# Value products of banded attention issued once per group of heads and query tile, with their sums in the exponentials' banks

## The chip, the cores and the metric

The kernel runs on one core of a Trainium2 chip. The metric is the time of one execution on the device, in microseconds, as the median of several runs. TensorE (PE) multiplies matrices into PSUM, where this kernel rotates eight banks, each of 128 partitions by 512 float32 numbers; its weight loads are shown as PEld. VectorE (DVE), ScalarE (ACT) and GpSimd (POOL) do the rest of the arithmetic. SyncE (SP) issues the DMAs, in order, in one queue.

## The reference

Two branches work on the same 2048 rows and are mixed by a gate. Branch A is attention with 32 heads of 16 numbers, in which a query sees itself and the 255 keys before it; branch B is a dense layer, gelu, and a second dense layer. The kernel is given everything in float32.

```python
g = sigmoid((x * gate_w).sum(-1, keepdims=True))          # x: 2048 x 512
q, k, v = split(x @ wqkv)                                 # 32 heads of 16
scores = q @ k.T / 4, kept where 0 <= query - key < 256, else -1e9
a = (softmax(scores) @ v) @ wo                            # wo: 512 x 512
b = gelu(x @ w1 + b1) @ w2 + b2                         # 512 -> 1792 -> 512
out = g * a + (1 - g) * b
```

## The kernel before

Dense products are made of three matmuls each (`mm3`, lines 95 to 97), on numbers split into a high and a low part, over query tiles of T = 512 rows (four tiles, `c` or `t`). The dense work is one long generator: queries, keys and values of all tiles (qk, v), then eight turns of the two dense layers, half of the 1792 columns at a time. A turn has seven first-layer products (u), each followed by a chain of gelu steps on ACT, DVE and POOL, then four second-layer products (y). At the end stand the attention's output products (a).

Attention goes over eight groups of four heads. For each group there are 16 blocks of 128 keys (`kb`), so 128 steps `u`; in each step PE does, for each of four heads `i`:

- `att_max` (m): a score matmul with queries as output rows into a bank "sm" (three of these). DVE takes the row maxima (M), eight blocks ahead of their use.
- `att_exp` (s): a score matmul with keys as output rows into a bank "st". ACT writes exp(scores) into "pt" buffers of SBUF, each for two heads, and POOL sets the corners outside the band to zero (`affine_select`, lines 427 and 430).
- `att_pvs` (p), at the third head: products of finished exponentials with values ("pv", line 455), in four column strips of 32, one for each head, accumulated over the key blocks of a query tile in one bank. At the last block of a tile ACT copies the bank to "nd" (line 466), which goes to DRAM as ND.
- `fill` (f): dense work, 2296 ns in each step, between the attention's matmuls.

A key block has 384 queries, so it feeds the query tile of its own and, for the last two blocks of a tile, also the next one. The kernel before issues pv at every second block: four pairs of block and tile at a tile's second block (two of them of the tile before it; two pairs in tile 0), two at its fourth.

After odd groups `att_norm` fetches sums (den) and numerators (num) from ND, takes the reciprocal on DVE (line 496), writes it to DRAM (RD), fetches it spread over rows (rb), multiplies (line 501) and writes OT. At the end `load_o` fetches OT, ACT and DVE split it (ot, lines 533 and 536), and `final` multiplies with wo.

The order on PE, ACT, DVE and POOL is the order in which the program is written out (`manual_schedule`). It is kept by a planned clock: `after(ns, ...)` puts a step off, `tick(ns)` moves the clock by the planned length of a matmul and runs what is due; `NORM` is the delay between the steps of `att_norm`. The DMAs on SP are ordered by the scheduler. Buffers are rotations by tag (`bufs`): whoever takes the next buffer waits until the one in it is no longer read.

Of the kernel before, what the change touches and what calls it, by code (L numbers as in the profile page):

```python
# [32 lines left out]
def gated_mix(ctx: ExitStack, tc: tile.TileContext, x, wqkv, wo, w1, b1, w2, b2, gate_w, out):  # L33
# [28 lines left out]

    identr = cp.tile([128, 128], F32R, name="identr")
    one = sb.tile([128, 128], F32, tag="x1", bufs=2, name="one")
    make_identity(nc, one)
    nc.vector.tensor_copy(identr, one)
    ident = f32(identr)
# [17 lines left out]
    nms = [cp.tile([128, RB, 32], F32R, name=f"nm{i}") for i in range(2)]  # L85
    for nm in nms:
        nc.gpsimd.memset(f32(nm), 0.0)
    vbuf = cp.tile([128, 2, NB * 68 + 16], F32, name="vbuf")
# [37 lines left out]
    def load_raw(key, early=False):  # L126
        kind, i = key
        src = {"qk": lambda: wk4[:, :, i * 128:(i + 1) * 128],
               "v": lambda: wqkv[i * 128:(i + 1) * 128, 2 * D:3 * D],
               "w1": lambda: w1k[:, :, i * 128:(i + 1) * 128],  # L130
               "w2": lambda: w2[i * 128:(i + 1) * 128],
               "wo": lambda: wo[i * 128:(i + 1) * 128]}[kind]()
        if early and kind == "v" and i < 2:
            raw = sb.tile([128, T], F32, tag="sq", bufs=2, name=f"raw_{kind}{i}")
        elif early and kind == "v":
            raw = f32(sb.tile([128, 2, T], F32R, tag="h", bufs=8, name=f"raw_{kind}{i}"))[:, 0]
        elif early:
            raw = sb.tile([128, 2, 384], F32, tag="pt", bufs=11, name=f"raw_{kind}{i}")
# [88 lines left out]
    def gate_z(t, b):  # L227
        xr = xrs.pop((t, b))
        junk = sb.tile([128, D], BF16, tag="x1", bufs=2, name=f"xj{t}_{b}")
        nb = t * NB + b  # L230
# [49 lines left out]
    def qkv(t):  # L280
# [17 lines left out]
        for n, (kind, j) in enumerate(pieces):  # L298
# [9 lines left out]
            if t == 0 and n == 10:  # L308
                nc.sync.dma_start(b2b, b2.partition_broadcast(128))
                nc.sync.dma_start(b1c, b1.rearrange("(f p) -> p f", p=128))  # L310
# [83 lines left out]
    def att_rows(g_, rb):  # L394

        need(*[("max", g_, rb * RB + b, i) for b in range(RB) for i in range(4)])
        m = Ms.pop((g_, rb))
        nm = nms[rb % 2][:, :, 0:8].rearrange("p b (i k) -> p k b i", k=2)
# [3 lines left out]
        tt = sb.tile([128, RB, 32], F32, tag="tt", bufs=2, name=f"tt{g_}_{rb}")  # L402
        nc.vector.transpose(tt.rearrange("p b c -> p (b c)"), f32(nms[rb % 2]).rearrange("p b c -> p (b c)"))

# [9 lines left out]
    def att_exp(g_, kb, i):  # L414
# [8 lines left out]
        nc.tensor.matmul(p[:, :w], ks[:, pr, s, kb * 128:(kb + 1) * 128],  # L423
# [17 lines left out]
    def att_pv(g_, kb, c):  # L441
# [6 lines left out]
        if first:  # L448
            n = g_ * NT + c - 1
            if n >= 0:  # L450
                need(("nd", *divmod(n, NT)))
            pvs[g_, c] = ps.tile([128, T], F32, tag="pv", bufs=1, name=f"pv{g_}_{c}")
        pv = pvs[g_, c]
        for i in range(4):
# [4 lines left out]
                             skip_group_check=True, tile_position=(0, 32 * i))  # L459
        tick((e - q) * 1.67 + 150)  # L460
        if kb % NB == NB - 1 and c == kb // NB:
            nd = sb.tile([128, T], F32, tag="tmp", bufs=4, name=f"nd{g_}_{c}")
            pv = pvs.pop((g_, c))
# [21 lines left out]
    def att_norm(t, c):  # L485

        v = ND[t][c].rearrange("g (i r) c -> (g i) r c", r=32)
        den = sb.tile([128, 32], F32, tag="den", bufs=2, name=f"den{t}_{c}")
        rec = sb.tile([128, 32], F32, tag="rec", bufs=2, name=f"rec{t}_{c}")
        nc.sync.dma_start(den, v[:, 16, :].rearrange("i (j c) -> i j c", c=32))  # L490
        num = sb.tile([128, T], F32, tag="tmp", bufs=4, name=f"num{t}_{c}")
        rb = sb.tile([128, T], F32, tag="tmp", bufs=4, name=f"rb{t}_{c}")
        nc.sync.dma_start(num, v[:, 0:16, :])

        def rcp():
            nc.vector.reciprocal(rec, den)
            nc.sync.dma_start(RD[t][c].rearrange("h (j c) -> (h j) c", c=32), rec)
            nc.sync.dma_start(rb, RD[t][c].unsqueeze(1).broadcast_to([8, 16, T]))
# [16 lines left out]
    def load_o(t):  # L515
# [7 lines left out]
        for c in range(NC):  # L523
            need(("o", t, c))
            if t == 0:
                raw = sb.tile([128, T], F32, tag=("x1", "sq")[c % 2], bufs=2, name=f"or{t}_{c}")
            else:
                raw = sb.tile([128, 2, 384], F32, tag="pt", bufs=11, name=f"or{t}_{c}")
                raw = raw.rearrange("p a b -> p (a b)")[:, 0:T]
# [39 lines left out]
    def mlp(n):  # L569
# [22 lines left out]
        for b in range(NB):  # L592
# [3 lines left out]
            p = ps.tile([128, D], F32, tag="d", bufs=2, name=f"y{t}_{half}{b}")  # L596
            if half == 1:
                ya = sb.tile([128, D], F32, tag="ya", bufs=2, name=f"ya{t}_{b}")
                need(("y", 0, t, b))
                nc.sync.dma_start(ya, YA[t][ts])  # L600
            for i in range(HF):
# [4 lines left out]
                if last and b == NB - 1 and later:  # L606
                    load(later.pop(0))
            def ev(p=p, b=b, ts=ts, ya=b2b if half == 0 else ya):
                y = sb.tile([128, D], F32, tag="y", bufs=1, name=f"yo{t}_{half}{b}")
                nc.vector.scalar_tensor_tensor(y, p, 0.5, ya, op0=ALU.mult, op1=ALU.add)  # L610
# [20 lines left out]
    def final(t):  # L631
# [8 lines left out]
        for b in range(NB):  # L640
            ts = slice(b * 128, (b + 1) * 128)
            nb = t * NB + b
            after(YLAND if nb == 0 else 0, scale_y, nb)
            a = sb.tile([128, 2, 384], F32, tag="pt", bufs=11, name=f"ao{nb}")
            a = a.rearrange("p a b -> p (a b)")[:, 0:D]
# [51 lines left out]
    for u in range(-LEAD, NU):  # L697
# [35 lines left out]
START = 117e3  # L733
NORM = 6000
GELU = (700, 1500, 2300, 3300, 4200, 5000)
# [29 lines left out]
```

## Time and profile before

| | us |
|---|---|
| median of three runs | 807.09 (806.85 to 811.15) |
| the profiled execution | 806.06 |
| its span, first to last instruction | 804.4 |
| PE busy in the span | 783.4 |
| DVE busy | 526.3 |
| ACT busy | 427.0 |
| POOL busy | 357.9 |

A line of a group reads: source line, engine, operation, output from inputs by the program's names, shapes, count, then busy time and the mean length of one in ns, then the engine's idle time before it and who ended it. In the timeline a row gives start, length, engine and line; consecutive instructions of one form are merged ("x16"). A matmul's length is modelled and matmuls overlap, so the step from one start to the next is the time that it takes. A pv product appears there as two records (1408 records for 704 products). A wait reads "who waited, for whom: us in total, times, longest us". A row of the windows gives, for a stretch of the span, the busy time of each engine, and its last line the sums.

### The profile page before, as it was taken

To read this page: it belongs to the slowest core of one execution; us is meant where nothing else is said; L and a number is where in the kernel's file an instruction comes from. 1 tells how busy PE (TensorE), PEld (TensorE's weight loads), DVE (VectorE), ACT (ScalarE), POOL (GpSimd) and SP (SyncE) were. 2 spreads that over 40 slices of the span, in tenths; PEclk is the share of its full clock that TensorE was granted. 3 is DMA by queue.
4 is the path that set the end of the run, shared out by engine and by line. 5 is a ranking of instruction groups with operands and counts; after the bars stand their busy time and mean duration, and the time that the engine had idled before them with its cause. 6 is when DMAs were issued, how large, how long until landed. Compare 5 with 4: busy or idle time off the path is not lost.

```text
span 804.4 us, 14522 instructions
## 1 busy us (share of the span) xinstructions
PE 783.4 (97%) x4630; PEld 612.9 (76%) x4630; DVE 526.3 (65%) x1517; ACT 427.0 (53%) x865; POOL 357.9 (44%) x702
## 2 busy tenths in 40 slices
PE   9999999989999999999999999999999999999988
PEld 6888888866777777777767867877787778776767
DVE  4532333997478757956895798568767966891353
ACT  4433423365467446745674576456646654775631
POOL 2200000156357544854674477437645753675100
PEclk9999999999999999999999999999999999999999
DMA  9985856636332544462235546432664374345863
GB/s 259 390 313 197 307 176 196 207 114 237 105 101 68 195 141 120 147 194 86 78 108 158 170 126 218 119 97 90 195 193 125 103 227 153 99 128 177 282 234 117
DMA packets 94925, 135.72 MB, mean 169 GB/s; under 512 B 32256, under 2 KB 43776, under 8 KB 94848
## 3 DMA queue, kind: packets, MB, share of 16 engines
q1 hardware_dynamic: 94848, 134.79, 52.5%
q8 instruction: 37, 0.61, 0.3%
q14 instruction: 40, 0.33, 0.1%
HBM read 79.70 MB, written 55.05 MB: 168 GB/s over the span
## 4 chain that ended last, share of the span: by engine, by line
PE 75%; DVE 12%; issue 4%; ACT 4%; POOL 3%; DMA 2%; SPq 0%; DVEq 0%; POOLq 0%; ACTq 0%
PE pv L455 9%; PE st L423 8%; PE sm L383 7%; PE y L95 6%; PE y L97 6%; PE y L96 5%; DVE jm L388 4%; PE u L95 4%; PE qk L95 4%; PE qk L97 4%; PE qk L96 4%; PE u L96 3%; PE u L97 3%; DVE sqh L552 2%; PE v L95 2%
## 5 line engine op out<-in xcount | busy, mean ns | idle before, releaser
L388 DVE CUSTOM_DVE_ANT_0 jm<-sm,mask 128x384 bf16<-128x384 f32 (+2 forms) x512 | 269.7, 527 | 129.7 <-PE sm L383 106.5
L435 ACT ACTIVATE pt<-st 128x384 f32<-128x384 f32 (+2 forms) x512 | 232.2, 471 | 194.8 <-PE st L423 189.6
L427 POOL TENSOR_SCALAR_AFFINE_SELECT pt<-pt 128x256 f32<-128x256 f32 x256 | 120.9, 472 | 203.9 <-ACT pt L435 199.3
L423 PE MATMUL st<-qs,ks 128*128 128x384 f32 (+2 forms) x512 | 172.2, 338 | 8.5 <-ACT pt L435 5.6
L383 PE MATMUL sm<-ks,qs 96*128 96x384 f32 (+2 forms) x512 | 169.5, 333 | 4.2 <-DVE M L388 4.0
L423 PEld LDWEIGHTS st<-qs,ks 128*128 128x128 f32 x512 | 97.2, 190 | 36.7 <-ACT pt L435 14.1
L383 PEld LDWEIGHTS sm<-ks,qs 96*128 96x128 f32 x512 | 96.4, 188 | 30.4 <-DVE M L388 8.9
L430 POOL TENSOR_SCALAR_AFFINE_SELECT pt<-pt 128x256 f32<-128x256 f32 x224 | 101.9, 455 | 0.0
L564 POOL TENSOR_TENSOR h<-x1h,h 128x512 fp32r<-128x512 f32 x56 | 75.4, 1346 | 42.3 <-DVE h L561 38.6
L455 PE MATMUL pv<-pt,vbuf 128*32 128x384 f32 (+2 forms) x1408 | 91.4, 388 | 0.1
L95 PE MATMUL y<-w,h 128*128 128x512 f32 x224 | 90.9, 406 | 0.0
L97 PE MATMUL y<-w,h 128*128 128x512 f32 x224 | 88.1, 393 | 0.9 <-POOL h L564 0.9
L96 PE MATMUL y<-w,h 128*128 128x512 f32 x224 | 87.8, 392 | 0.0
L408 POOL CAST qs<-tt 8x256 fp32r<-8x256 f32 x128 | 60.5, 473 | 50.5 <-PE u L97 39.2
L95 PE MATMUL u<-mx,w 128*128 128x512 f32 x196 | 80.5, 411 | 0.0
L96 PE MATMUL u<-mx,w 128*128 128x512 f32 x196 | 76.8, 392 | 0.0
L97 PE MATMUL u<-mx,w 128*128 128x512 f32 x196 | 76.6, 391 | 0.0
L455 PEld LDWEIGHTS pv<-pt,vbuf 128*32 128x32 f32 x1408 | 38.3, 109 | 36.9 <-issue 17.2
L555 ACT ACTIVATE sqh<-sqh 128x512 f32<-128x512 f32 x56 | 35.3, 631 | 46.5 <-DVE sqh L552 46.2
L552 DVE SCALAR_TENSOR_TENSOR sqh<-sqh,x1h 128x512 f32<-128x512 f32 x56 | 53.0, 946 | 2.3 <-ACT sqh L549 1.6
L250 DVE TENSOR_TENSOR qke<-qk,qke 128x512 fp32r<-128x512 f32 x32 | 22.1, 690 | 49.5 <-ACT qke L247 45.4
L95 PEld LDWEIGHTS y<-w,h 128*128 128x128 f32 x224 | 42.4, 189 | 11.8 <-issue 11.1
(118 smaller groups left out, 1186.2 us busy)
## 6 DMA issues: line engine op xcount, KB each, us to landing
mx<-XT SPq DMA_DIRECT2D x24, 512.0 KB
SQ<-qke SPq DMA_DIRECT2D x16, 512.0 KB
SK<-qke SPq DMA_DIRECT2D x16, 512.0 KB
qs<-SQ SPq DMA_DIRECT2D x64, 128.0 KB
ND<-nd SPq DMA_DIRECT2D x32, 256.0 KB
ks<-SK SPq DMA_DIRECT2D x60, 128.0 KB
raw_w<-in_B_w_dram SPq DMA_DIRECT2D x28, 256.0 KB
SV<-vx SPq DMA_DIRECT2D x16, 272.0 KB
```

The lines of the kernel that those rows point to most:

```text
L95: nc.tensor.matmul(p, lh, rh, start=first, stop=False)
L96: nc.tensor.matmul(p, lh, rl, start=False, stop=False)
L97: nc.tensor.matmul(p, ll, rh, start=False, stop=last)
L383: nc.tensor.matmul(p[:, :w], qs[0:96, pr, b * 128:(b + 1) * 128], ks[0:96, pr, s, k0:k0 + w], start=True, stop=True)
L388: nc.vector.tensor_tensor_reduce(junk[:, :w], p[:, :w], mask[:, 384 - w:384], 1.0, -3e38, ALU.add, ALU.max, M[:, b % RB, i:i + 1])
L423: nc.tensor.matmul(p[:, :w], ks[:, pr, s, kb * 128:(kb + 1) * 128], qs[:, pr, kb * 128:kb * 128 + w], start=True, stop=True)
L427: nc.gpsimd.affine_select(out=pt[:, :, 0:128], in_=pt[:, :, 0:128], pattern=[[0, 2], [1, 128]], compare_op=ALU.is_ge, fill=0.0, base=0, ch ...
L430: nc.gpsimd.affine_select(out=pt[:, :, 256:384], in_=pt[:, :, 256:384], pattern=[[0, 2], [-1, 128]], compare_op=ALU.is_ge, fill=0.0, base= ...
L435: nc.scalar.activation(pt[:, s, :w], p[:, :w], AF.Exp, scale=SCALE)
L455: nc.tensor.matmul(pv[32 * i:32 * i + 32, q - c * T:e - c * T], vt[:, 68 * (kb % NB) + 17 * i:68 * (kb % NB) + 17 * i + 32], pts[g_, kb, i ...
L552: nc.vector.scalar_tensor_tensor(sq, sq, GC, x1, op0=ALU.add, op1=ALU.mult)
L564: nc.gpsimd.tensor_sub(h[:, 1], x1, f32(h[:, 0]))
```

## The change

- pv is issued once per group of heads and query tile, at the tile's fourth block, for up to six key blocks in one go (`att_pvs`).
- The pv bank no longer has a bank of its own: it is taken from the tag "st", which gets three banks instead of two.
- The rotation of exponentials "pt" has 14 buffers instead of 11. Room comes from: the bias b2, which was held in SBUF all the time (`b2b`), and is now fetched by a DMA into a "ya" buffer before each output of the first half; one "nm" and one "tt" buffer instead of two; three "tmp" buffers instead of four (the fourth block of x goes to "raw"); y outputs in the tag "sq" (the tag "y" goes); no copy of the identity matrix; the reciprocal in place (`rec` goes); the early value weights in the "xt" buffer.
- The value load of a tile is issued at the tile's first block rather than at the third block of the tile before.
- The planner's clock counts 0.8 ns per column and 40 ns for a pv product (1.67 and 150 before), and `NORM` is 4500 ns (6000 before).

```diff
-    identr = cp.tile([128, 128], F32R, name="identr")
...
-    b2b = cp.tile([128, D], F32, name="b2b")
...
+    nms = cp.tile([128, RB, 32], F32R, name="nm")
...
-            xrs[t, b] = sb.tile([128, D], F32, tag="tmp", bufs=4, name=f"xr{t}_{b}")
+            xrs[t, b] = sb.tile([128, D], F32, tag=("tmp", "raw")[b // 3], bufs=3, name=f"xr{t}_{b}")
...
-            pts[g_, kb, pr] = sb.tile([128, 2, 384], F32, tag="pt", bufs=11, name=f"pt{g_}_{kb}_{pr}")
+            pts[g_, kb, pr] = sb.tile([128, 2, 384], F32, tag="pt", bufs=14, name=f"pt{g_}_{kb}_{pr}")
...
-        p = ps.tile([128, 384], F32, tag="st", bufs=2, name=f"st{g_}_{kb}_{i}")
+        p = ps.tile([128, 384], F32, tag="st", bufs=3, name=f"st{g_}_{kb}_{i}")
...
-            pvs[g_, c] = ps.tile([128, T], F32, tag="pv", bufs=1, name=f"pv{g_}_{c}")
+            pvs[g_, c] = ps.tile([128, T], F32, tag="st", bufs=3, name=f"pv{g_}_{c}")
...
-        tick((e - q) * 1.67 + 150)
+        tick((e - q) * 0.8 + 40)
...
         g_, kb = divmod(u, NKB)
-        if kb % 2 == 0:
-            return
         c, k = divmod(kb, NB)
-        blocks = [kb - 1, kb]
-        if k == 1 and c > 0:
-            blocks = [kb - 3, kb - 2] + blocks
-        for b in blocks:
-            att_pv(g_, b, c)
+        if k == NB - 1:
+            for b in range(max(kb - 5, 0), kb + 1):
+                att_pv(g_, b, c)
...
-            nc.vector.reciprocal(rec, den)
-            nc.sync.dma_start(RD[t][c].rearrange("h (j c) -> (h j) c", c=32), rec)
+            nc.vector.reciprocal(den, den)
+            nc.sync.dma_start(RD[t][c].rearrange("h (j c) -> (h j) c", c=32), den)
...
-            if half == 1:
-                ya = sb.tile([128, D], F32, tag="ya", bufs=2, name=f"ya{t}_{b}")
+            ya = sb.tile([128, D], F32, tag="ya", bufs=2, name=f"ya{t}_{half}{b}")
+            if half == 0:
+                nc.sync.dma_start(ya, b2.partition_broadcast(128))
+            else:
...
-                y = sb.tile([128, D], F32, tag="y", bufs=1, name=f"yo{t}_{half}{b}")
+                y = sb.tile([128, D], F32, tag="sq", bufs=2, name=f"yo{t}_{half}{b}")
...
-        if u % NB == 2 and -NB < u < NU - NB:
-            att_load_v(*divmod(u // NB + 1, NT))
+        if u % NB == 0 and u >= 0:
+            att_load_v(*divmod(u // NB, NT))
...
-NORM = 6000
+NORM = 4500
```

How PE's order moves, in the first group of heads at query tile 1 (blocks 4 to 7; in a name like `pt_5_1` stand the block and the pair of heads, in `st_6_2` the block and the head). Before, after the tile's second block, block 5:

```order
L423 MATMUL st_6_2_2002<-qs,ks 128x384
L455 MATMUL pv_1_2005<-pt_2_0_1719,vbuf 32x128 x2
L455 MATMUL pv_1_2005<-pt_2_1_1754,vbuf 32x128 x2
L455 MATMUL pv_1_2005<-pt_3_0_1787,vbuf 32x256 x2
L455 MATMUL pv_1_2005<-pt_3_1_1829,vbuf 32x256 x2
L455 MATMUL pv_1_2005<-pt_4_0_1857,vbuf 32x384 x2
L455 MATMUL pv_1_2005<-pt_4_1_1881,vbuf 32x384 x2
L455 MATMUL pv_1_2005<-pt_5_0_1930,vbuf 32x384 x2
L455 MATMUL pv_1_2005<-pt_5_1_1958,vbuf 32x384 x2
L95 MATMUL y_01_1945<-w_4_1733,h_4_1641 128x512
```

The changed kernel at the same place:

```order
L417 MATMUL st_6_2_1997<-qs,ks 128x384
L90 MATMUL y_01_1938<-w_4_1724,h_4_1631 128x512
L91 MATMUL y_01_1938<-w_4_1724,h_4_1631 128x512
L92 MATMUL y_01_1938<-w_4_1724,h_4_1631 128x512
L377 MATMUL sm_14_2_2004<-ks,qs 128x384
L417 MATMUL st_6_3_2007<-qs,ks 128x384
```

The group is gone from here. It stands two blocks later, behind `st_8_2`, where before only blocks 6 and 7 (256 and 128 columns) stood:

```order
L449 MATMUL pv_1_2100<-pt_2_0_1710,vbuf 32x128 x2
L449 MATMUL pv_1_2100<-pt_2_1_1745,vbuf 32x128 x2
L449 MATMUL pv_1_2100<-pt_3_0_1764,vbuf 32x256 x2
L449 MATMUL pv_1_2100<-pt_3_1_1812,vbuf 32x256 x2
L449 MATMUL pv_1_2100<-pt_4_0_1838,vbuf 32x384 x2
L449 MATMUL pv_1_2100<-pt_4_1_1863,vbuf 32x384 x2
L449 MATMUL pv_1_2100<-pt_5_0_1923,vbuf 32x384 x2
L449 MATMUL pv_1_2100<-pt_5_1_1953,vbuf 32x384 x2
L449 MATMUL pv_1_2100<-pt_6_0_1976,vbuf 32x256 x2
L449 MATMUL pv_1_2100<-pt_6_1_1996,vbuf 32x256 x2
L449 MATMUL pv_1_2100<-pt_7_0_2019,vbuf 32x128 x2
L449 MATMUL pv_1_2100<-pt_7_1_2048,vbuf 32x128 x2
```

Twelve rows, 48 records in the profile, stand in one piece where there were two pieces of eight and four. Behind them follow three dense matmuls, `st_8_3`, more dense work, `st_9_0` and `st_9_1`; the last of these takes the bank that pv held.

On DVE, at the end of the program, between the outputs of tile 0 (ao) and the split attention outputs of tile 1 (ot). Before:

```order
L658 SCALAR_TENSOR_TENSOR ao_9559<-a_2_0_9560,g,yb_1_9503 128x512
L658 SCALAR_TENSOR_TENSOR ao_9582<-a_3_0_9583,g,yb_1_9503 128x512
L536 TENSOR_TENSOR ot_0_9513<-or_0_9517,ot_0_9513 128x512
L501 TENSOR_TENSOR num_3_9429<-num_3_9429,rb_3_9430 128x512
L536 TENSOR_TENSOR ot_1_9514<-or_1_9519,ot_1_9514 128x512
L496 RECIPROCAL rec_3_9568<-den_3_9567 128x32
L536 TENSOR_TENSOR ot_2_9515<-or_2_9521,ot_2_9515 128x512
L536 TENSOR_TENSOR ot_3_9516<-or_3_9523,ot_3_9516 128x512
```

And in the changed kernel:

```order
L490 TENSOR_TENSOR num_3_9421<-num_3_9421,rb_3_9422 128x512
L649 SCALAR_TENSOR_TENSOR ao_9572<-a_2_0_9573,g,yb_1_9511 128x512
L485 RECIPROCAL den_3_9564<-den_3_9564 128x32
L649 SCALAR_TENSOR_TENSOR ao_9591<-a_3_0_9592,g,yb_1_9511 128x512
L525 TENSOR_TENSOR ot_0_9521<-or_0_9525,ot_0_9521 128x512
L525 TENSOR_TENSOR ot_1_9522<-or_1_9527,ot_1_9522 128x512
L525 TENSOR_TENSOR ot_2_9523<-or_2_9529,ot_2_9523 128x512
L525 TENSOR_TENSOR ot_3_9524<-or_3_9531,ot_3_9524 128x512
```

The product and the reciprocal of the normalisation stand earlier, and the four ot's in one piece.

More of the change, by code (lines that the diff above doesn't have):

```diff
@@ L60, in gated_mix @@
     YB = [dr.tile([T, D], F32, name=f"YB{t}") for t in range(NT)]
-    identr = cp.tile([128, 128], F32R, name="identr")
[L64 to L67, printed above, removed]
+    ident = sb.tile([128, 128], F32, tag="x1", bufs=2, name="ident")
+    make_identity(nc, ident)
     gwb = sb.tile([128, D], F32, tag="ya", bufs=2, name="gwb")
-    b2b = cp.tile([128, D], F32, name="b2b")
     b1c = cp.tile([128, NF], F32, name="b1c")
@@ L84, in gated_mix @@
                                 fill=1.0, base=-k, channel_multiplier=1)
-    nms = [cp.tile([128, RB, 32], F32R, name=f"nm{i}") for i in range(2)]
-    for nm in nms:
-        nc.gpsimd.memset(f32(nm), 0.0)
+    nms = cp.tile([128, RB, 32], F32R, name="nm")
+    nc.gpsimd.memset(f32(nms), 0.0)
     vbuf = cp.tile([128, 2, NB * 68 + 16], F32, name="vbuf")
@@ L132, in load_raw @@
                "wo": lambda: wo[i * 128:(i + 1) * 128]}[kind]()
[L133 to L136, printed above, removed]
+        if early and kind == "v":
+            if i == 0:
+                raws["v"] = f32(sb.tile([128, NC, 2, T], F32R, tag="xt", bufs=1, name="raw_v"))
+            raw = raws["v"][:, i, 0]
         elif early:
-            raw = sb.tile([128, 2, 384], F32, tag="pt", bufs=11, name=f"raw_{kind}{i}")
+            raw = sb.tile([128, 2, 384], F32, tag="pt", bufs=14, name=f"raw_{kind}{i}")
             raw = raw.rearrange("p a b -> p (a b)")[:, 0:T]
@@ L607, in mlp, with ev @@
                     load(later.pop(0))
[L608 to L609 removed]
+            def ev(p=p, b=b, ts=ts, ya=ya):
+                y = sb.tile([128, D], F32, tag="sq", bufs=2, name=f"yo{t}_{half}{b}")
                 nc.vector.scalar_tensor_tensor(y, p, 0.5, ya, op0=ALU.mult, op1=ALU.add)
```

22 lines of the change are left out of this document (10 added, 12 removed).

## The prediction

> **What bounds the kernel now.** I read the page first (busy shares, granted clock, chain), then the windows by stage, then TensorE's timeline around the groups of value products, and last the waits.
>
> ```profile
> span 804.4 us, 14522 instructions
> ...
> PE 783.4 (97%) x4630; PEld 612.9 (76%) x4630; DVE 526.3 (65%) x1517; ACT 427.0 (53%) x865; POOL 357.9 (44%) x702
> ...
> PEclk9999999999999999999999999999999999999999
> ...
> PE 75%; DVE 12%; issue 4%; ACT 4%; POOL 3%; DMA 2%; SPq 0%; DVEq 0%; POOLq 0%; ACTq 0%
> PE pv L455 9%; PE st L423 8%; PE sm L383 7%; PE y L95 6%; PE y L97 6%; PE y L96 5%; DVE jm L388 4%; PE u L95 4%; PE qk L95 4%; PE qk L97 4%; PE qk L96 4%; PE u L96 3%; PE u L97 3%; DVE sqh L552 2%; PE v L95 2%
> ```
>
> TensorE (PE) is busy for 97% of the span at full granted clock and carries 75% of the chain. A busy PE is not a PE at its peak, so what counts is the distance between the starts of its matmuls. The largest single line of the chain is L455, the products of exponentials with values (pv), 9% of the span. VectorE (DVE) is second with 12%. Where it matters shows in the windows: the first answer below sums the seven stretches in which the dense work is the first layer (u), the second sums the eight of the second layer (y).
>
> ```profile
> sum 270.00, PE 263.38 PEld 203.54 DVE 228.72 ACT 181.77 POOL 172.79; mean PE 37.63 PEld 29.08 DVE 32.67 ACT 25.97 POOL 24.68
> ...
> sum 299.00, PE 295.15 PEld 228.32 DVE 182.62 ACT 151.93 POOL 156.07; mean PE 36.89 PEld 28.54 DVE 22.83 ACT 18.99 POOL 19.51
> ```
>
> In the y stretches PE is 98.7% busy and DVE 61%: a nanosecond taken off PE there is off the end. In the u stretches DVE is at 85% and PE idles for 6.6 of 270 us.
>
> **Term 1: half of the borders between dense work and pv groups go.** Today the 22 pairs of block and query tile per group of heads are issued at every second block, 8 times, so 64 pv groups in all; the change issues them at every fourth block, 32 groups. The matmuls stay the same in number and shape; what goes is 32 times the cost of entering and leaving. TensorE's timeline (start, length, records merged) prices it; the three pv rows are of three places.
>
> ```profile
> 178.35 0.34 PE L423 MATMUL st<-qs,ks 128*128 128x384 f32 x1
> ...
> 179.39 0.33 PE L423 MATMUL st<-qs,ks 128*128 128x384 f32 x1
> 179.65 1.50 PE L455 MATMUL pv<-pt,vbuf 128*32 128x384 f32 x16
> 181.08 0.50 PE L95 MATMUL u<-xt,w 128*128 128x512 f32 x1
> 181.42 0.40 PE L96 MATMUL u<-xt,w 128*128 128x512 f32 x1
> 181.65 0.39 PE L97 MATMUL u<-xt,w 128*128 128x512 f32 x1
> ...
> 182.40 0.34 PE L423 MATMUL st<-qs,ks 128*128 128x384 f32 x1
> 182.58 0.39 PE L95 MATMUL u<-xt,w 128*128 128x512 f32 x1
> ...
> 199.38 2.15 PE L455 MATMUL pv<-pt,vbuf 128*32 128x128 f32 x32
> 201.46 0.50 PE L95 MATMUL y<-w,h 128*128 128x512 f32 x1
> ...
> 209.12 0.86 PE L455 MATMUL pv<-pt,vbuf 128*32 128x256 f32 x16
> 209.91 0.50 PE L95 MATMUL y<-w,h 128*128 128x512 f32 x1
> ```
>
> - Entering: from a score matmul's start to the next start is 0.18 us before dense work (182.40 to 182.58) and 0.26 before pv (179.39 to 179.65): 0.08.
> - The first matmul after pv holds PE for 0.34 us (181.08 to 181.42), the next one 0.23 (181.42 to 181.65): 0.11.
> - The groups themselves: 16 records of 384 columns take 1.43 us (179.65 to 181.08), 16 of 256 and 128 columns 0.79 (209.12 to 209.91), together 2.22. The same 32 records in one group take 2.08 (199.38 to 201.46): 0.14 less.
>
> Together 0.33 us for each group that is joined to another, times 32: **10.6 us**. The inner steps could not shrink further, and without the 0.14 (if joining wide to narrow gains nothing) it is 6.1; I take 10.6, since 2.08 against 2.22 is measured on the shapes that get joined.
>
> **Term 2: a third bank for the exponentials.** Scores for the exponentials (st) now have two PSUM banks, so a score matmul waits until the exponential two before it is done.
>
> ```profile
> PE st L423 <- ACT pt L435: 5.6, 11, 1.2
> PE sm L383 <- DVE M L388: 4.0, 5, 1.8
> ...
> PEld st L423 <- ACT pt L435: 14.1, 28, 1.5
> ...
> ACT sqh L555 <- DVE sqh L552: 46.2, 41, 2.8
> ...
> L466 ACT ACTIVATE nd<-pv 128x512 f32<-128x512 f32 x32 | 19.1, 598 | 7.1 <-PE pv L455 7.1
> ```
>
> PE itself stood 5.6 us in 11 such waits; the weight loads' 14.1 us are an outer bound, as part of that runs beside matmuls. With one bank more, PE may go one st interval further, which is 1.04 us (178.35 to 179.39), and only the longest wait (1.2) exceeds that. But ACT is late because a tanh ahead of the exponentials waits for DVE (46.2 us, 41 times), and PE, let through, meets DVE next at the maxima (L383, 4.0 us already). Between nothing and 14.1 I take **3.0 us**, about half of 5.6: the row of PE itself is the nearest. The pv bank joins this rotation, so it fills one of three places while a group runs. That is no tighter than today: pv then waits for the exponential for which the third-next score would wait anyway.
>
> **Term 3: one long group instead of two short ones.** A joined group is 0.79 + 2.08 - 0.14 = 2.73 us, against at most 2.08 now, and for its length DVE and ACT get no new scores. In u stretches DVE has 15% to spare, about 2.7 us of a tile's 17.8 (the 569 us of both answers over 32 tiles), more than the 0.65 us by which the group is longer. Bounds: nothing, and 15 tiles (270 parts in 569 of 32) times 0.65 = 10 us. Taken: **+2.5 us**, nearer to nothing because DVE's spare time is four times the gap. PE's order of everything else is kept, and DVE's order differs by a place or two, since the planner counts a shorter time for pv.
>
> **Term 4: the end.** After the last pv group the final products wait for split attention outputs (ot); DVE has normalisation work between them.
>
> ```profile
> 765.51 0.75 DVE L658 SCALAR_TENSOR_TENSOR ao<-a,g,yb 128x512 f32<-128x512 f32 x1 [2.34 <-PE a L97]
> 766.17 0.68 DVE L536 TENSOR_TENSOR ot<-or,ot 128x512 fp32r<-128x512 f32 x1
> 766.77 0.68 DVE L501 TENSOR_TENSOR num<-num,rb 128x512 f32<-128x512 f32 x1
> 767.38 0.68 DVE L536 TENSOR_TENSOR ot<-or,ot 128x512 fp32r<-128x512 f32 x1
> 767.98 0.34 DVE L496 RECIPROCAL rec<-den 128x32 f32<-128x32 f32 x1
> 768.24 1.22 DVE L536 TENSOR_TENSOR ot<-or,ot 128x512 fp32r<-128x512 f32 x2
> ...
> PE a L97 <- DVE ot L536: 2.1, 4, 1.5
> ```
>
> PE idles 2.1 us here. With NORM at 4500 the product at 766.77 and the reciprocal at 767.98 come ahead of the previous output, so the ot's follow one another: up to 0.6 + 0.26 us sooner (the start distances). Bounds: 2.1 gained, and 1 lost if a reordered load is late; taken **0.5 us** gained.
>
> **Edits costed at nothing, and what covers them.**
>
> ```profile
> L610 DVE SCALAR_TENSOR_TENSOR yo<-y,ya 128x512 f32<-128x512 f32 x16 | 11.0, 687 | 19.4 <-PE y L97 19.3
> L610 DVE SCALAR_TENSOR_TENSOR yo<-y,b2b 128x512 f32<-128x512 f32 x16 | 10.8, 678 | 0.0
> ...
> SPq L370 <- PE pv L455: 37.1, 14, 4.6
> ...
> q1 hardware_dynamic: 94848, 134.79, 52.5%
> ```
>
> The bias b2 is loaded anew for each of 16 outputs of the first half, 128 x 512 numbers of 4 bytes each: 15 loads more (the single one goes), 3.9 beside 134.79 MB, with queues 52.5% full. The second half already loads its addend (ya) at the same place, and its 16 additions waited for PE, never for that load. The value load (vbuf) is issued at the tile's first block for a first use four blocks later, as before; it waits on SP for the pv group that frees its half, as today (37.1 us, 14 times). Behind it on SP stand key and query loads of the next heads and raw weights; the former have eight blocks of lead. If this cover goes, an exponential or a gelu step queued on ACT behind a late weight split waits, and PE with it. Fewer copies of tiles (nm, tt, tmp) are reused a whole tile of blocks later; the shorter NORM delays put the product of one tile before the next tile's loads.
>
> Sum: -10.6 - 3.0 + 2.5 - 0.5 = **-11.6 us**. The profiled execution took 806.06 us (span 804.4), so 794.5 on its scale; it stands 1.0 us below the median of the three runs, so I predict 795.5. A measurement of this kernel tells about 0.5%, 4 us, from no change.
>
> **Rivals.**
>
> 1. *VectorE sets the pace of the u stretches.* Then borders removed there return as waits for maxima, and so does term 2. Gain: 17 of 32 borders, 5.6 us: 801.5 on the median's scale. For it: 85% DVE, and DVE's 12% of the chain. Against: PE is still 97.5% busy there. Chance 0.17.
> 2. *Nothing is given back*: the waits for exponentials and those at the end vanish whole and term 3 costs nothing: 10.6 + 5.6 + 2.1 = 18.3 us, 789. For it: waits of at most 1.2 us against one more interval of 1.04. Against: DVE's lateness behind them stays. Chance 0.17.
> 3. *The pv bank is held too long (slower).* After a group the third score matmul needs pv's bank, evacuated by ACT in 598 ns. PE reaches it after two rounds of dense work and scores, about 2 x 1.04 us. If ACT, in order, is held by more than 1.5 us at that point in most tiles (its longest wait for DVE is 2.8), each tile pays about 0.6 us: 19 us, 815 with the rest of the sum kept. Against: 22 of ACT's 32 evacuations stood waiting for PE's group to end, thus nothing is ahead of them. Chance 0.05. The Trainium skill, TensorEngine Tiling (Array Packing), section Performance Considerations, warns in this sense that after a fourfold tiling the PSUM copy may become the bottleneck; by that rule the time would be this rival's. The trace disagrees so far: the copy takes 19.1 us in all, and it waits for PE.
> 4. *New queueing on SP or ACT eats the gain* (late raw weights, b2 loads): 803 to 808. Chance 0.06.
> 5. *The borders don't go with the groups* (the step between shapes inside a joined group costs what a border costs): terms 2 to 4 remain, about 806. Against: 2.08 for three shapes in one group. Chance 0.03.
>
> My forecast, 791 to 800 as its own range, has 0.52. Faster by over 0.5% are forecast and rivals 1 and 2: 0.86; within 0.5%: most of rivals 4 and 5, 0.09; slower 0.05. The range 788.5 to 802 leaves out 4, 5, 3 and part of 2.
>
> **What would show it.** Right: 32 pv groups, those of full tiles near 2.7 us; starts inside them spaced as now; st's waits for pt below half of 5.6 us; PE's row busier in y stretches and these shorter by about 0.3 us per tile. Term 3 wrong: PE's waits for DVE M grow well beyond 4.0 us, DVE idle during pv. Rival 3: score matmuls waiting for nd. Rival 4: ACT waiting for raw_w or SP for OT or ND. The prediction fails as a whole if waits of a kind not in the rows above (vbuf, den) enter PE's chain.

## The result and the profile after

The changed kernel took **795.16 us** (median of six runs, 794.96 to 797.51); the kernel before took 807.66 in the same session. One of its six runs lies far off at 1527.54 us; without it the median is 807.09. The ratio is 0.985, with a 95% interval of 0.9824 to 0.9876. The prediction was 795.5 us, range 788.5 to 802, faster with a chance of 0.86. The profiled execution of the changed kernel was its longest run, 797.51 us (span 795.8; the other spans were 793.2 to 794.7), so what its trace shows need not hold for all runs. The two profiled executions differ by 8.6 us in their spans, the medians by some 12.

The page of the changed kernel, same rows as before:

```profile
span 795.8 us, 14526 instructions
...
PE 770.4 (97%) x4630; PEld 616.6 (77%) x4630; DVE 530.0 (67%) x1516; ACT 423.3 (53%) x865; POOL 363.7 (46%) x701
...
PE 78%; DVE 10%; issue 5%; DMA 3%; ACT 2%; POOL 2%; SPq 0%; DVEq 0%; POOLq 0%
...
q1 hardware_dynamic: 97008, 138.72, 55.2%
```

PE is still busy for 97%, and its share of the chain rose from 75% to 78%. The time was not moved to another engine as a whole. The b2 loads show in the queue: 138.72 MB instead of 134.79, the 3.9 MB that the prediction counted.

TensorE's timeline at a joined group of a full tile (columns: start, duration, engine and line, operation, count):

```profile
439.46 0.33 PE L417 MATMUL st<-qs,ks 128*128 128x384 f32 x1
439.73 2.80 PE L449 MATMUL pv<-pt,vbuf 128*32 128x128 f32 x48
442.45 0.50 PE L90 MATMUL y<-w,h 128*128 128x512 f32 x1
442.79 0.40 PE L91 MATMUL y<-w,h 128*128 128x512 f32 x1
```

From the group's first start to the next dense matmul are 442.45 - 439.73 = 2.72 us; the prediction composed 2.73. The step before the group (0.27 where an undisturbed score takes 0.177) and the first step after it (0.34 where a dense matmul takes 0.227) are what they were.

I added up, over the whole trace, by how much the distance between the starts of neighbouring matmuls exceeds that of an undisturbed pair of the same kind. This counts lost time whatever the profile calls it:

| us, profiled executions | before | after | difference |
|---|---|---|---|
| pv groups | 64 | 32 | |
| step into a group, all groups | 6.6 | 3.4 | -3.2 |
| inside, to the next other matmul's start | 87.0 | 82.1 | -4.9 |
| first step behind | 7.0 | 3.5 | -3.5 |
| excess ahead of scores for the exponentials (st) | 14.6 | 7.0 | -7.6 |
| excess ahead of scores for the maxima (sm) | 6.4 | 17.2 | +10.7 |
| excess ahead of dense matmuls | 13.7 | 15.3 | +1.6 |

The sum is -6.9, against -8.6 in the spans; start-up accounts for 0.7 of the rest, and about 1 us stays unplaced. So 19.2 us were taken off PE (11.6 with the groups, 7.6 ahead of the exponentials' scores), and some 12 came back. They came back mainly in the u stretches: counted there alone, the excess ahead of the maxima rose from 5.8 to 14.8 us and the one ahead of the exponentials fell from 11.0 to 4.5; in the y stretches the maxima's rose only from 1.4 to 2.9. The waits of the changed kernel (us in total, times, longest) say where:

```profile
PE sm L377 <- DVE M L382: 11.4, 15, 1.8
PE a L92 <- DVE ot L525: 3.8, 3, 2.4
PE st L417 <- ACT nd L460: 0.2, 1, 0.2
PEld st L417 <- ACT pt L429: 0.8, 3, 0.4
PEld sm L377 <- DVE M L382: 23.6, 33, 2.2
ACT sqh L544 <- DVE sqh L541: 64.1, 46, 3.2
ACT nd L460 <- PE pv L449: 43.2, 22, 2.5
DVE den L485 <- DMA den<-ND: 3.2, 1, 3.2
```

PE's own wait for exponentials (5.6 us before) is not listed any more, and the weight loads' is 0.8 instead of 14.1. In its place PE waits for the maxima: 11.4 us in 15 waits instead of 4.0 in 5. Tanh (sqh), too, waits longer for DVE: 64.1 instead of 46.2.

By stretches of dense work, the u stretches together fell from 304.1 to 299.8 us and the y stretches from 300.4 to 294.0. The end, from the first final product to the last instruction, grew from 50.6 to 53.4 in this execution.

### The profile page after: what moved, and what is told of

It is laid out like the page before. It is cut to its first block, busy times and chain, and to the rows that moved or that the text cites. A ratio compares the mean times of both kernels' runs of the same rounds, so it can differ in the third digit from the quotient of the medians.

```text
span 795.8 us, 14526 instructions
## 1 busy us (share of the span) xinstructions
PE 770.4 (97%) x4630; PEld 616.6 (77%) x4630; DVE 530.0 (67%) x1516; ACT 423.3 (53%) x865; POOL 363.7 (46%) x701
## 3 DMA queue, kind: packets, MB, share of 16 engines
q1 hardware_dynamic: 97008, 138.72, 55.2%
## 4 chain that ended last, share of the span: by engine, by line
PE 78%; DVE 10%; issue 5%; DMA 3%; ACT 2%; POOL 2%; SPq 0%; DVEq 0%; POOLq 0%
PE pv L449 9%; PE st L417 9%; PE sm L377 8%; PE y L90 6%; PE y L92 6%; PE y L91 5%; PE u L90 4%; DVE jm L382 4%; PE u L91 4%; PE u L92 4%; PE qk L92 4%; PE qk L90 4%; PE qk L91 4%; PE v L90 2%; PE v L92 2%
## 5 line engine op out<-in xcount | busy, mean ns | idle before, releaser
L429 ACT ACTIVATE pt<-st 128x384 f32<-128x384 f32 (+2 forms) x512 | 229.0, 472 | 132.3 <-PE st L417 127.8
L421 POOL TENSOR_SCALAR_AFFINE_SELECT pt<-pt 128x256 f32<-128x256 f32 x256 | 126.7, 495 | 190.2 <-ACT pt L429 184.6
L377 PE MATMUL sm<-ks,qs 96*128 96x384 f32 (+2 forms) x512 | 170.8, 335 | 12.2 <-DVE M L382 11.4
L417 PE MATMUL st<-qs,ks 128*128 128x384 f32 (+2 forms) x512 | 169.4, 333 | 2.2 <-POOL qs L402 1.9
L424 POOL TENSOR_SCALAR_AFFINE_SELECT pt<-pt 128x256 f32<-128x256 f32 x224 | 101.4, 453 | 0.0
L553 POOL TENSOR_TENSOR h<-x1h,h 128x512 fp32r<-128x512 f32 x56 | 73.0, 1304 | 38.1 <-DVE h L550 30.8
L402 POOL CAST qs<-tt 8x256 fp32r<-8x256 f32 x128 | 64.0, 500 | 49.4 <-PE u L92 38.2
L449 PE MATMUL pv<-pt,vbuf 128*32 128x384 f32 (+2 forms) x1408 | 84.3, 386 | 0.1
L449 PEld LDWEIGHTS pv<-pt,vbuf 128*32 128x32 f32 x1408 | 41.5, 110 | 42.0 <-issue 28.9
L544 ACT ACTIVATE sqh<-sqh 128x512 f32<-128x512 f32 x56 | 35.3, 631 | 64.2 <-DVE sqh L541 64.1
```

Source lines behind the costliest of these rows:

```text
L377: nc.tensor.matmul(p[:, :w], qs[0:96, pr, b * 128:(b + 1) * 128], ks[0:96, pr, s, k0:k0 + w], start=True, stop=True)
L402: nc.gpsimd.tensor_copy(dst, tt[32 * i:32 * i + 8].unsqueeze(1).broadcast_to([8, 2, RB, 32]))
L421: nc.gpsimd.affine_select(out=pt[:, :, 0:128], in_=pt[:, :, 0:128], pattern=[[0, 2], [1, 128]], compare_op=ALU.is_ge, fill=0.0, base=0, ch ...
L424: nc.gpsimd.affine_select(out=pt[:, :, 256:384], in_=pt[:, :, 256:384], pattern=[[0, 2], [-1, 128]], compare_op=ALU.is_ge, fill=0.0, base= ...
L429: nc.scalar.activation(pt[:, s, :w], p[:, :w], AF.Exp, scale=SCALE)
L449: nc.tensor.matmul(pv[32 * i:32 * i + 32, q - c * T:e - c * T], vt[:, 68 * (kb % NB) + 17 * i:68 * (kb % NB) + 17 * i + 32], pts[g_, kb, i ...
```

## The experiments

All edits are made on the changed kernel. "Two groups" stands for the rule of before, which groups blocks in pairs. Ratios are to the kernel before in the session of the run. It took 806.70 us beside e1 to e4, 806.36 beside e5 to e8, 809.29 beside e9 to e11 and 807.16 beside e12, so medians of different sessions can mislead by 2 to 3 us, and the ratios are the better comparison.

| experiment | groups a tile | pv's bank | NORM | median us | ratio (95%) |
|---|---|---|---|---|---|
| changed kernel | 1 | st's three | 4500 | 795.16 | 0.985 (0.9824 to 0.9876) |
| e1 two groups | 2 | own | 4500 | 812.51 | 1.0062 (1.0038 to 1.0086) |
| e2 own bank | 1 | own | 4500 | 797.80 | 0.9882 (0.9861 to 0.9903) |
| e3 sm bank | 1 | sm's four | 4500 | 799.14 | 0.9896 (0.9875 to 0.9917) |
| e4 late reciprocal | 1 | st's three | 4500 | 798.82 | 0.9892 (0.9861 to 0.9924) |
| e5 four groups | 4 | own | 4500 | 820.33 | 1.0157 (1.0137 to 1.0178) |
| e6 two, old price | 2 | own | 4500 | 812.67 | 1.0064 (1.0045 to 1.0083) |
| e7 joined, old price | 1 | st's three | 4500 | 800.18 | 0.9905 (0.9877 to 0.9932) |
| e8 split on GpSimd | 1 | st's three | 4500 | 794.55 | 0.9846 (0.9815 to 0.9877) |
| e9 two, long delay | 2 | own | 6000 | 804.65 | 0.9947 (0.993 to 0.9963) |
| e10 joined, long delay | 1 | st's three | 6000 | 799.98 | 0.9884 (0.9869 to 0.9899) |
| e11 e8 and e10 together | 1 | st's three | 6000 | 795.85 | 0.9839 (0.982 to 0.9859) |
| e12 last sums on ACT's queue | 1 | st's three | 4500 | 797.65 | 0.9886 (0.9858 to 0.9914) |

**e1: two groups again, everything else as changed.**

```diff
-        if k == NB - 1:
-            for b in range(max(kb - 5, 0), kb + 1):
-                att_pv(g_, b, c)
+        if kb % 2 == 0:
+            return
...
+        blocks = [kb - 1, kb]
+        if k == 1 and c > 0:
+            blocks = [kb - 3, kb - 2] + blocks
+        for b in blocks:
+            att_pv(g_, b, c)
...
```

Besides this, st has two banks and pv its own, and the value load stands at its old place.

> The changed kernel with the value products issued at every second block again, in 64 groups, their bank their own and two banks for the exponentials' scores, the value load at its old place. All shared buffers, the 14 exponential buffers, NORM and the planner's prices stay. Theory 'borders' (32 borders of 0.33 us make the gain, the rest cancels): 795.2 + 10.6 = about 806, level with before. Rival 'buffers' (third bank, 14 buffers and the new order of the other engines make half of it or more): 801 or less.

812.51 us. The gain is gone without the joined groups, but the kernel is also slower than before, by more than either theory said. So the rest of the edits, costed at nothing, cost 5.8 us here. DVE's waits for transfers in this run (of these three, the kernel before has none):

```profile
DVE num L494 <- DMA rb<-RD: 11.6, 5, 3.2
DVE den L489 <- DMA den<-ND: 9.0, 2, 5.8
...
DVE yo L605 <- DMA ya<-YA: 6.7, 1, 6.7
```

One of them in the timelines of SP, then DVE, then PE:

```profile
579.81 0.32 SPq L606 DMA_DIRECT2D YB<-yo  x1
...
580.70 0.60 SPq L491 DMA_DIRECT2D rb<-RD  x1
```

```profile
585.73 0.69 DVE L494 TENSOR_TENSOR num<-num,rb 128x512 f32<-128x512 f32 x1 [3.15 <-DMA rb<-RD]
```

```profile
586.82 0.45 PE L377 MATMUL sm<-ks,qs 96*128 96x384 f32 x1 [0.97 <-DVE M L382]
```

The reciprocals' rows (rb) were asked for on SP behind an output of the dense work (and a load of keys); DVE, in order, stood 3.15 us for them with maxima queued behind, and PE stood for a maximum.

**e2: joined groups, but two banks for st and an own one for pv.**

```diff
-        p = ps.tile([128, 384], F32, tag="st", bufs=3, ...
+        p = ps.tile([128, 384], F32, tag="st", bufs=2, ...
-            pvs[g_, c] = ps.tile([128, T], F32, tag="st", bufs=3, ...
+            pvs[g_, c] = ps.tile([128, T], F32, tag="pv", bufs=1, ...
```

> The changed kernel with only the banks as before: one for the value products, two for the exponentials' scores; groups stay joined. Theory 'borders, third bank cancels': PE's idle time before score matmuls for the exponentials comes back (0 to about 5 us) and that before the maxima falls from 11.4 to about 4 to 6 us; time 794 to 797. Rival 'the third bank is worth its waits': 3 to 6 us slower, 798 to 801.

797.80 us, between the two bands. By medians of two sessions the third bank is worth 2.6 us, by ratios 0.3%; the two intervals overlap a little, so the gain is not shown beyond the noise. The waits of PE in this run:

```profile
PE sm L377 <- DVE M L382: 7.2, 11, 1.8
...
PE st L417 <- ACT pt L429: 1.9, 4, 0.6
```

The excess ahead of st is 12.5 us (7.0 with the third bank), that ahead of sm 10.9 (17.2). The bank takes 5.5 from the one and adds 6.3 to the other: in the profiled executions it only moves the wait.

**e3: the pv bank in the maxima's rotation.** The fourth place goes to sm (and pv) instead of st.

```diff
+        p = ps.tile([128, 384], F32, tag="sm", bufs=4, name=f"sm{g_}_{b}_{i}")
...
+            pvs[g_, c] = ps.tile([128, T], F32, tag="sm", bufs=4, ...
...
+        p = ps.tile([128, 384], F32, tag="st", bufs=2, ...
```

> The changed kernel with the joined bank in the rotation of the maxima's scores (four banks, the value products among them), two for the exponentials' scores. If VectorE's pace in the first-layer stretches is what PE meets, more room ahead of VectorE doesn't help: PE's waits for maxima fall by no more than the waits for exponentials rise (0 to about 5 us), time 794 to 798. If it is the number of banks there, the 11.4 us before maxima mostly vanish and the time falls to 787 to 791.

799.14 us, a little above the first band and far from the second. The waits of PE turned over:

```profile
PE st L417 <- ACT pt L429: 12.8, 17, 1.8
...
PE sm L377 <- DVE M L382: 0.8, 1, 0.8
```

Waits for M and for pt together are 11.4 in the changed kernel, 9.1 in e2 and 13.6 here. Where the banks go decides mostly what PE waits for, and much less how long.

**e4: the last tile's reciprocal and product put off by 4500 on the planner's clock.**

```diff
+        late = 4500 if (t, c) == (NT - 1, NC - 1) else 0
-        after(NORM, rcp), after(3 * NORM, mul)
+        after(NORM + late, rcp), after(3 * NORM + late, mul)
```

> The changed kernel with the last tile's reciprocal and product put off by 4.5 us on the planner's clock, so that VectorE does the split attention outputs of tile 1 before it waits for the last sums. If VectorE's wait for that load (3.2 us) is what held PE at the end (2.4 us idle and some 1.6 us at a lower granted clock after it), the end gets 3 to 4 us shorter: 791 to 792.5. If the wait only moves to the next products, 794 to 796.

798.82 us, above both bands, so no gain. DVE's 3.15 us wait for den went, but the products' outputs came later, and PE idled further on, for a later ot (3.2 us at most, against 2.4):

```profile
PE a L92 <- DVE ot L526: 4.6, 3, 3.2
```

That is 4.6 us at the end against 3.8. The wait was moved down the chain of the last normalisation, not taken away.

**e5: four groups a tile** (e1 with `blocks = [kb]`, and the two blocks before with it at a tile's first).

> The experiment with two value groups per tile, now with four: after every block the value products of that block (and, at a tile's first block, of the two blocks that reach into it); 128 groups instead of 64, all else as there. Borders: 64 more at 0.33 us are 21 us above its 812.5, so 831 to 836, with entry and post of about 0.09 and 0.11 us each unchanged. Rival, VectorE's pace: where VectorE or ScalarE sets the time, borders are hidden; then the waits for M fall by as much as the borders grow and the time stays at 817 to 826.

820.33 us, within the rival's band and 11 us below that of the borders alone. From e1 to e5 the 64 added groups cost what they should on PE: into and behind them 26.5 us instead of 13.6, inside 98.5 instead of 87.4, together +24. But the excess ahead of sm fell from 11.9 to 5.5, of st from 13.2 to 7.2 and of dense matmuls from 15.9 to 11.6, -16.5 together. The time rose by 7.8.

```profile
PE sm L377 <- DVE M L382: 3.5, 2, 1.8
...
PE st L417 <- ACT pt L429: 0.6, 2, 0.4
```

The rival's mechanism is shown: a border's time on PE is also time in which DVE and ACT catch up. A border costs PE 24 / 64 = 0.38 us here and 11.6 / 32 = 0.36 in the change itself, but these 64 cost only 0.12 us each of the kernel's time.

**e6 and e7: the planner's price of a value product as before**, with two groups and with joined ones.

```diff
-        tick((e - q) * 0.8 + 40)
+        tick((e - q) * 1.67 + 150)
```

> The experiment with two value groups per tile, and the planner's price of a value product as before (1.67 ns a column + 150 instead of 0.8 + 40). Theory 'prices': the 5.8 us by which two groups stood above the kernel before come from the lower price, by which the planner fits more dense work and maxima beside a tile than VectorE can do; then 805 to 808, and PE's waits for M back from 8.7 to below 6 us. Rival 'rest of the edits' (shorter NORM, shared buffers, b2 loads, later value load): 811 to 814 as there.

> The changed kernel with the planner's price of a value product as before (1.67 ns a column + 150), all else as changed. If the low price is what puts PE in front of VectorE's maxima (11.4 us of waits against 4.0 before): waits for M below 7 us and 789 to 793 us. If those waits come from the joined groups and the third bank themselves: waits for M stay at 10 to 13 us and 794 to 797. If the price fits a joined group (2.7 us, against 1.73 us by the low price and 4.2 by the old one): slower, 797 to 800.

812.67 us: the price is not what makes two groups slow; this "prices" theory fell. With joined groups 800.18 us, at the edge of the last of the three cases: the lower price belongs to the gain, by 4 to 5 us (by ratios and by medians; the intervals just don't touch). A part of it may be the clock, as these four runs stood at mean granted clocks of 0.994 to 0.998. PE's waits for M did not fall with it (12.9 us), and DVE stood for transfers again:

```profile
DVE num L490 <- DMA rb<-RD: 17.2, 5, 7.2
```

**e8: the weights' low parts on GpSimd instead of DVE.**

```diff
-        after(LAND, split, key, nc.vector)
+        after(LAND, split, key, nc.gpsimd)
```

> The changed kernel with the low parts of the weights (a subtraction per raw weight, about 0.6 us each) on GpSimd instead of VectorE. Theory: PE, let through by fewer borders and a third bank, is now held by VectorE's pace (waits for M 11.4 us by PE, 17 us from start to start); then these waits fall below 6 us and the time to 787 to 792. Rival: GpSimd, slower at it and busy with query copies and masks, is late itself; PE then waits for w, qs or pt from GpSimd, and the time stays at 794 to 798 or rises to 805.

794.55 us, the same as the changed kernel within the intervals; the rival's first band. PE's waits:

```profile
PE st L417 <- POOL qs L402: 4.9, 4, 1.6
PE a L92 <- DVE ot L525: 4.6, 3, 3.3
PE sm L377 <- DVE M L382: 4.6, 7, 1.8
PE y L92 <- POOL h L553: 3.7, 5, 1.4
```

Waits for M fell from 11.4 to 4.6, as the theory said, and those for GpSimd (qs, h) rose from 3.8 to 8.6. The u stretches became 4.8 us shorter (295.0), the y stretches 3.3 longer (297.3), and the end 0.9 longer. So DVE did pace the u stretches of the changed kernel; freeing it paid there and was spent elsewhere.

**e9, e10, e11: NORM at 6000 as before**, with two groups, with joined ones, and with joined ones and e8's edit.

```diff
-NORM = 4500
+NORM = 6000
```

> The experiment with two value groups per tile, and the normalisation's delay NORM at 6000 as before. Theory 'early normalisation': the 5.8 us by which two groups stood above the kernel before come from VectorE, which works in order and stood 27 us for DMAs of the normalisation and of ya (num for rb 11.6, den for ND 9.0, yo for ya 6.7; none of these three before); with the longer delay these fall below 6 us and the time to 805 to 808. Rival, the other edits (shared buffers, b2 loads, fewer copies): 810 to 814 as there, VectorE's waits for DMAs small or not.

> The changed kernel with NORM at 6000 as before. Theory 'early normalisation' for the joined groups: its waits of VectorE for DMAs are 6.9 us (den 3.2, num 2.3, yo 0.7, the rest as before), and the 2.4 us idle of PE at the first late ot goes with den's: 792 to 794.5. If the shorter delay is worth what the prediction's fourth term said (products ahead of the last output): 795.5 to 797.5. If it matters nowhere: 794.8 to 795.6.

> The changed kernel with the low parts of the weights on GpSimd and NORM at 6000. If the gains add (0.6 us of the one, 1 to 3 of the other): 791 to 793.5, waits for M near 4.6 us. Rival: NORM at 6000 puts the products of the last tile into the end, where ot is waited for; 794 to 797.

With two groups 804.65 us, 7.9 less than e1 by medians, 1.15% by ratios: the theory of the early normalisation holds there. DVE's waits for rb, den and ya are gone from the trace; the only transfers that it still waits for (3.6 us, qke) lie in the projections ahead.

With joined groups the longer delay did not help: 799.98 us, outside all three bands that were expected. In its session the kernel before was slower too; the ratio, 0.9884 against 0.985, makes it 2.7 us more than the changed kernel, with intervals that overlap a little. Up to the u stretch that begins near 446 us the trace goes with the changed kernel's to within 1 us, and at the first final product it is 1.9 us behind. Most of that comes about at one place of this stretch, in PE's timeline:

```profile
478.08 0.44 PE L377 MATMUL sm<-ks,qs 96*128 96x384 f32 x1 [1.43 <-DVE M L382]
...
479.25 0.68 PE L377 MATMUL sm<-ks,qs 96*128 96x384 f32 x1
...
480.18 3.37 PE L449 MATMUL pv<-pt,vbuf 128*32 128x384 f32 x32
```

About 1.2 us behind the wait the steps double: the group takes 3.37 us, in e12, behind the same wait, 2.15, and from the end of the wait to the next dense matmul 5.40 us pass instead of 3.82. The granted clock from 476 to 484 us is 0.79 in e10 and 1.00 in e12 and in the changed kernel. So these 1.6 us are the clock's and not the delay's order of work. In the end PE idles 2.86 us for a late ot, with another slow stretch behind it. The mean granted clock of e10's four runs was 0.991 to 0.996, that of the changed kernel's six 0.997 to 1.0, so a part of the difference is the clock in these runs too. What the delay itself is worth here is not shown. e11 gives 795.85, in the rival's band, so the gains don't add; it is not told apart from the changed kernel.

**e12: the last sums issued from ACT's queue.**

```diff
-                nc.sync.dma_start(ND[c][g_ // 2][g_ % 2], nd)
+                q = nc.scalar if (g_, c) == (2 * NT - 1, NC - 1) else nc.sync
+                q.dma_start(ND[c][g_ // 2][g_ % 2], nd)
```

> The changed kernel with one transfer moved: the last group's sums (nd to ND) are issued from ScalarE's queue, right behind the copy that makes them, instead of SP's. Theory: in the changed kernel the end is bound by SP's order, not by PE. The last copy ended at 743.2, but its transfer was issued at 747.83, behind one (rb) that waits for another's landing (RD), and den followed at 752.62; moved, ND is issued near 743.3, den lands before VectorE reaches the reciprocal, the 3.2 us wait for den, the 2.44 us idle of PE and the slow stretch behind it go, and the last ot comes up to 4 us sooner (PE's idle there is 1.04): 790.5 to 793, the end from the first final product under 51 us. Rival: the chain behind (rb, the second product, its way out and back) is held by SP's order anyway, or the end is PE's: 794 to 796, the end 52.5 to 53.5 us.

The reason for it stands in the changed kernel's timelines of SP, DVE and PE at the end:

```profile
746.17 0.60 SPq L487 DMA_DIRECT2D rb<-RD  x1
...
747.83 0.38 SPq L461 DMA_DIRECT2D ND<-nd  x1
...
752.62 0.60 SPq L479 DMA_DIRECT2D den<-ND  x1
```

```profile
754.90 0.35 DVE L485 RECIPROCAL den<-den 128x32 f32<-128x32 f32 x1 [3.15 <-DMA den<-ND]
...
755.74 2.49 DVE L525 TENSOR_TENSOR ot<-or,ot 128x512 fp32r<-128x512 f32 x4
```

```profile
756.47 0.50 PE L92 MATMUL a<-wo,ot 128*128 128x512 f32 x1 [2.44 <-DVE ot L525]
```

Moved, ND was issued at 743.50, but SP reached den only at 748.11, since rb stands ahead of it too:

```profile
745.46 0.60 SPq L488 DMA_DIRECT2D rb<-RD  x1
...
748.11 0.60 SPq L480 DMA_DIRECT2D den<-ND  x1
```

```profile
754.26 0.35 DVE L486 RECIPROCAL den<-den 128x32 f32<-128x32 f32 x1 [2.25 <-DMA den<-ND]
```

DVE's wait fell only from 3.15 to 2.25, PE's idle from 2.44 to 1.53. The end was 50.9 us long in the profiled execution, 2.5 shorter than the changed kernel's, as the theory had it; about 1.6 of that is the stretch of doubled steps shown further below, which e12's profiled execution (mean granted clock 1.0) doesn't have. The six runs say otherwise: 797.65 us (795.39 to 801.05), above both bands. The shorter end is seen in one trace; a gain in time is not shown. No experiment gave a version that is told apart from the changed kernel as faster.

## Why the prediction was right, step by step

- **Term 1, borders (-10.6): right, as PE's time.** Step counting gives -11.6. The three parts came as composed: entry halved (-3.2), first step behind halved (-3.5), and the shared parts inside a joined group (-4.9 against 32 x 0.14 = 4.5). Rival 5, that the border stays inside the group, fell.
- **Term 2, third bank (-3.0): in keeping with e2's 2.6, which is not told apart from nothing; wrong in what was seen.** PE's own waits for exponentials went whole, as rival 2 had it (excess -7.6, of which e2 gives the bank 5.5), and came back at the maxima.
- **Term 3, the long group (+2.5): the step that was mis-sized.** I had named its failing sign: PE's waits for M well beyond 4.0. They are 11.4, and the excess ahead of sm grew by 10.7. e2 shows that the third bank brings the larger part of it (10.9 with an own bank, 17.2 with three). The rest is not shown to be the long group's either, as e1, with short groups, has 11.9. e8 shows that DVE's pace is behind it: with less work on DVE the waits for M fall from 11.4 to 4.6. I weighed a group's length against DVE's spare time within a tile. But PE meets DVE where it arrives early, in the u stretches (excess ahead of the maxima 14.8 us there, 5.8 before), and much of what PE gains there ends as such a wait. That is rival 1's mechanism. With 19.2 us gross and some 12 given back, rivals 1 and 2 were both at work and nearly cancelled: terms 2 and 3 came to -7.6 + 10.7 = +3.1 instead of -0.5.
- **Term 4, the end (-0.5): wrong sign in the profiled execution.** The end grew by 2.8 us (53.4 against 50.6), 2.44 of it PE's idle ahead of the first late ot and 1.6 a slow stretch behind it. The step that failed is "a reordered load is late", bounded by 1 us. In-order SP made the transfer of the last sums wait for another's landing. The spans of the other five runs are 1.1 to 2.6 us shorter than the profiled one.
- **Edits costed at nothing: wrong, and hidden by the joining.** I wrote that the shorter delays only move a product ahead of loads. With two groups they cost 7.9 us (e1 against e9). With the joined groups the same delay costs nothing that is seen (e10 is no faster). The price of a product, also taken as nothing, is worth 4 to 5 us with joined groups (e7) and nothing with two (e6). e9 also shows that what is left of the other edits is not a loss: two groups with the old delay are at 0.9947, faster than before. Which of these edits gains was not tried.
- **Rival 3, pv's bank held too long: fell.** Scores waited for nd once, 0.2 us, and 22 of ACT's evacuations stood waiting for the group's end, for 43.2 us, so the copy was hardly ever late. Rival 4's place (SP, DVE behind transfers) was real in e1, e6 and e7, but not in the changed kernel, apart from its end.

So the mechanism of term 1 is right, and that the time came out within 0.4 us is luck: the terms behind it are not of the forecast sizes, and the edits taken as nothing are worth several us. With NORM at 6000, joining and the third bank together bring 0.9947 to 0.9884, 0.6%; with 4500, 1.0062 to 0.985, 2.1%. Open is why the joined kernel bears the early normalisation (6.2 us of such waits of DVE) and the two-group kernel does not (27.3). e1 has the value load at its old place on SP beside the groups, and the two were not tried apart. Open is also what the delay is worth with joined groups, as e10's time is in part the clock's.

## What to carry to other kernels

Price a border from the distances between starts, but count it as gain only as far as the next engine lets PE through: here 0.36 to 0.38 us a border on PE, and from 0.12 (e1 to e5) to 0.46 (e2 to e1, 14.7 us for 32, with the value load's place changed too) of the kernel's time, depending on what else was late. A delay or planner's price that looks free deserves a row of its own: look for what stands ahead of the moved step on the in-order queue (SP, then DVE) and what is queued behind it. When a wait vanishes from the profile, add up the starts of all kinds of matmuls before calling it gained.

## What the runs showed of the hardware

After the 2.44 us in which PE stood, its steps doubled for a while. The changed kernel's PE timeline, and its windows (length, PE busy, granted clock, DMA share, GB/s):

```profile
757.27 0.39 PE L92 MATMUL a<-wo,ot 128*128 128x512 f32 x1
757.50 0.59 PE L90 MATMUL a<-wo,ot 128*128 128x512 f32 x1
757.88 0.63 PE L91 MATMUL a<-wo,ot 128*128 128x512 f32 x1
...
760.87 0.43 PE L92 MATMUL a<-wo,ot 128*128 128x512 f32 x1
```

```profile
750.00:758.00 8.00, 5.56 (x24) 0.97 0.84 271
758.00:766.00 8.00, 8.00 (x31) 0.82 0.87 290
```

From 757.50 to 760.87, 3.4 us, the step was 0.43 us instead of 0.227, and the window's granted clock 0.82. That costs about 8 x 0.2 = 1.6 us beside the idle itself. The Trainium skill, TensorE: Matmul & The Clock Gate, section Part 1: The HAM clock gate, has half clock after an idle window of about 3.4 us and full clock after as long a busy time, with 0.427 us a step of 512 columns. Step and recovery agree with this trace. The idle time does not: 2.44 us were enough here, and in e4 even a wait of 1.41, while e1's 2.65 us had no slow stretch behind it. PE timeline of e4, then of e1:

```profile
708.75 0.45 PE L377 MATMUL sm<-ks,qs 96*128 96x384 f32 x1 [1.41 <-DVE M L382]
...
709.26 0.63 PE L90 MATMUL y<-w,h 128*128 128x512 f32 x1
709.68 0.63 PE L91 MATMUL y<-w,h 128*128 128x512 f32 x1
```

```profile
771.79 0.50 PE L92 MATMUL a<-wo,ot 128*128 128x512 f32 x1 [2.65 <-DVE ot L529]
772.13 0.39 PE L90 MATMUL a<-wo,ot 128*128 128x512 f32 x1
```

So a wait of PE well below 3.4 us can cost more than its own length, but not each time: the same wait of 1.43 us near 477 us had doubled steps behind it in e10 and none in e12, and in e11 they followed waits of 0.53 and 0.75 us (granted clock 0.79 from 476 to 484 us). The spread of one kernel's runs goes with this in part: in e12 the run at a mean granted clock of 1.0 took 795.39 us and that at 0.994 took 801.05, but one at 0.998 took 798.90. In e5, whose waits for M and pt are the shortest, all four runs stood at 1.0 and within 1.3 us.
